# Attention steps between matmul half chunks: the two exponentials of each softmax, from neighbouring half chunks to half chunks two apart

## The chip, the cores and the metric

One Trainium2 chip, one of its cores. The metric is the device time of one execution in microseconds (us); the time before is the median of 3 runs, 785.88 us (785.31 to 786.62). A profile of one execution is there beside it.

## What is computed

For each of 8 batches and 8 heads, 32 learned queries `p` attend over 576 positions, and the 576 queries `q` then attend over the 32 packed rows. The result, 4608 tokens by 512, goes through a gated layer with a hidden width of 1536.

```python
def sm_attn(qq, kk, vv):
    s = scale * np.matmul(qq, kk.transpose(0, 1, 3, 2))
    s = s - np.max(s, axis=-1, keepdims=True)
    a = np.exp(s)
    a = a / (np.sum(a, axis=-1, keepdims=True) + 1e-09)
    return np.matmul(a, vv)
p_packed = sm_attn(p, k, v)            # first softmax: over 576 keys
out = sm_attn(q, p_packed, p_packed)   # second softmax: over 32 rows
g = x @ w_gate                         # x: out as (4608, 512)
silu = g * (1.0 / (1.0 + np.exp(-g)))
val = x @ w_val
return (silu * val @ w_out)
```

## The kernel before, in words

The attention's last product is folded into the first weights: `m_part` multiplies the packed rows (`ppts`) with the gate and value weights, and the layer's first products take the softmax weights `a2` themselves. High and low parts (`mh`/`ml`, `a2h`/`a2l`, `hh`/`hl`, `wo_h`/`wo_l`) are kept so that each product is three matmuls.

**Chunks.** The hidden width is 12 chunks (`fc`) of 128. `gv_chunk` does one chunk for half of a batch's tokens: half **A** has 256 columns, half **B** 320. This text calls the halves of chunk 9 **9A** and **9B**. In a half chunk TensorE fills two PSUM banks of the tag `gv` (the gate's, then the value's; the tag has two banks in all), ScalarE reads the first with the silu into `sg` (one buffer), VectorE multiplies the second bank by it into `hf` (in B also a 64-column rest into `t4`), ScalarE casts `hf` to `hh`, and VectorE takes the rest `hl`. The second product (`out_mm`) of a half chunk stands one chunk later. So on TensorE a half chunk is 12 matmuls into `gv` and 6 into `acc`. The first matmul of the next half chunk needs the bank which the silu reads, its seventh the bank that VectorE reads. On ScalarE the silu writes `sg` only when VectorE has read the half chunk before.

**Attention of the next batch.** While batch b is in the layer, `aux_of(b)` does the attention of batch d = b + 1, cut by `yield` into steps. A step is taken after each half's `out_mm`, so two to a chunk, in chunks 1 to 10; what is left is run off in chunk 11. In odd chunks `m_part` stands between the matmuls of half A and its `out_mm`, with two casts (`mh`) on ScalarE and two subtractions (`ml`) on VectorE.

- Step 1 and the step after: `q_scores`, the first softmax's scores in two groups. Each group has 16 small matmuls (L285; the trace shows 32), two maxima (`z`, L294) and two subtractions (`e`, L295) on VectorE, and one exponential (L298).
- Steps 4 and 5: `q_weights` sums the two groups (L308); step 5 then sends maxima and sums through DRAM (`zd`, `x`, L312 and L314, on SP's queue), and step 7 begins the join of the four parts (`y`, L319 and on).
- Steps 13 and 14: `s2_scores`, the second softmax's scores, transposed by VectorE into `s2`. From step 15 on come its two halves: maximum and subtraction (`s2_max`, L388 and L389), exponential (`s2_exp`, L393), sum and reciprocal (`s2_sums`, L400 to L402), scaling (L406), transposition and split (`s2_back`, L412 to L415).

**What sets the order.** TensorE's program is in the order of the code. On the other engines a scheduler sets it, but instructions that went through `pin` keep their order among themselves. An exponential is not issued in its step: it is put into the list `late`, and each `gv_chunk` takes one entry from the list right behind its silu:

```python
        nc.scalar.activation(sg[:, :n], pgs[0][:, :n], AF.Silu)
        if late:
            late.pop(0)()
```

Exponential and silu lie in different tables of ScalarE, so a table load (ACT_TABLE_LOAD) stands ahead of the exponential and another ahead of the next silu. Batch 0 and the attention of batch 1 run by a list written out by hand, which the change does not touch; `aux_of` serves batches 2 to 7, two softmaxes each.

Of the kernel before, what the change touches and what calls it, by code (L numbers as in the profile page):

```python
# [41 lines left out]
def tile_pack_attention_swiglu(ctx: ExitStack, tc: tile.TileContext, qT, kT, v, vq, pT, wgv, wout, out):  # L42
# [30 lines left out]
    def pin(ins):  # L73

        return tc.keep_in_program_order(ins) if steady[0] else ins

    late = []

    def ps():
        turn[0] += 1  # L80
        if wide[0] and turn[0] % 2:
            return ps_acc.tile([P, 512], F32, tag="acc", name="acc_aux")
        if wide[0]:
            return ps_gv.tile([P, 512], F32, tag="gv", name="gv_aux")
        return ps_aux.tile([P, 512], F32, tag="aux", name="aux")
# [126 lines left out]
    def s1_exp(b, par):  # L212
        t1, rs, nm = st1[b]
        nc.scalar.activation(
            t1[:, par], t1[:, par], AF.Exp, bias=nm[:, 1, par : par + 1], scale=SCALE, accum_out=rs[:, 0, par : par + 1]
        )
# [54 lines left out]
    def q_scores(b):  # L271


        k_t, p_t = kps[b]
        e = pool.tile([P, NPAR, NHP, NKQ * NP], F32, tag="s2", bufs=1, name="e1")
        z = pool.tile([P, 2, NPAR, NHP], F32, tag="z1", bufs=2, name="z1")
        sq[b] = (e, z)
        nc.gpsimd.memset(e[:, :, :, SQ:], 0.0)
        for g in range(2):
            pss = [ps(), ps()]  # L280
            for i in range(2):
                for j in range(NJ):
                    for par in range(NPAR):
                        r = slice(64 * par, 64 * par + 64)
                        nc.tensor.matmul(  # L285
                            pss[par][NP * j : NP * j + NP, i * SQ : (i + 1) * SQ],
                            p_t[r, 2 * g + i, :],
                            k_t[r, j // 2, 2 * g + i, j % 2 * SQ : j % 2 * SQ + SQ],
                            start=True, stop=True,
                        )  # L290
            hs = slice(2 * g, 2 * g + 2)
            for par in range(NPAR):
                x, m = pss[par][:, : 2 * SQ].rearrange("p (h n) -> p h n", h=2), z[:, 0, par, hs]
                pin(nc.vector.tensor_reduce(m, x, axis=AX.X, op=ALU.max))  # L294
                pin(nc.vector.tensor_tensor(  # L295
                    e[:, par, hs, :SQ], x, m.unsqueeze(2).broadcast_to([P, 2, SQ]), op=ALU.subtract
                ))
            late.append(lambda hs=hs: pin(nc.scalar.activation(e[:, :, hs, :SQ], e[:, :, hs, :SQ], AF.Exp, scale=SCALE)))  # L298
            yield

    def q_weights(b):


        e, z = sq[b]
        for g in range(2):
            yield
            hs = slice(2 * g, 2 * g + 2)
            pin(nc.vector.tensor_reduce(z[:, 1, :, hs], e[:, :, hs, :SQ], axis=AX.X, op=ALU.add))  # L308
        zv = z.rearrange("p s r h -> p s (r h)")
        x = pool.tile([P, NJ, 2, H], F32, tag="x1", bufs=1, name="x1")  # L310
        zd = dram.tile([P, 2, H], F32, tag="zd", bufs=2, name="zd")
        nc.sync.dma_start(zd, zv)  # L312
        for i in range(NJ):
            nc.sync.dma_start(x[NP * i : NP * i + NP], zd.rearrange("(j n) s h -> n j s h", j=NJ))  # L314
        for _ in range(2):
            yield
        y = pool.tile([P, 3, NJ + 1, H], F32, tag="pp", bufs=1, name="y1")
        m, t, f = y[:, 2, 0], y[:, 2, 1], y[:, 2, 2]
        pin(nc.vector.tensor_reduce(m, x[:, :, 0].rearrange("p j h -> p h j"), axis=AX.X, op=ALU.max))  # L319
        pin(nc.vector.tensor_tensor(  # L320
            y[:, 0, :NJ], x[:, :, 0], m.unsqueeze(1).broadcast_to([P, NJ, H]), op=ALU.subtract
        ))
        pin(nc.vector.tensor_tensor(y[:, 0, NJ], zv[:, 0], m, op=ALU.subtract))
        late.append(lambda: pin(nc.scalar.activation(y[:, 0], y[:, 0], AF.Exp, scale=SCALE)))
        yield
        pin(nc.vector.tensor_tensor(y[:, 1, :NJ], y[:, 0, :NJ], x[:, :, 1], op=ALU.mult))
        pin(nc.vector.tensor_reduce(t, y[:, 1, :NJ].rearrange("p j h -> p h j"), axis=AX.X, op=ALU.add))
        pin(nc.vector.tensor_scalar(f, t, 1e-9, None, op0=ALU.add))
        pin(nc.vector.reciprocal(t, f))
        pin(nc.vector.tensor_tensor(f, t, y[:, 0, NJ], op=ALU.mult))  # L330
        yield
        a1 = pool.tile([P, NPAR, NHP, NKQ, NP], F32, tag="a1", bufs=1, name="a1")
        for par in range(NPAR):
            w = e[:, par, :, :SQ]
            pin(nc.vector.tensor_tensor(
                w, w, f[:, NHP * par : NHP * par + NHP].unsqueeze(2).broadcast_to([P, NHP, SQ]), op=ALU.mult
            ))
            pin(nc.vector.transpose(
                a1[:, par].rearrange("p h k n -> p (h k n)"), e[:, par].rearrange("p h n -> p (h n)")
            ))  # L340
            yield
        sq[b] = a1
# [14 lines left out]
    def s2_tiles(b):  # L357
        st2[b] = (
            pool.tile([P, 2, NPAR, HS], F32, tag="s2", bufs=1, name="s2"),
            pool.tile([P, 3, 2 * NPAR * NBK], F32, tag="r2", bufs=1, name="r2"),  # L360
        )
# [14 lines left out]
    def s2_view(b, cs):  # L376
        s2, r2 = st2[b]
        n = NPAR * NBK
        rows = slice(cs.start * n, cs.stop * n)
        return (  # L380
            s2[:, cs].rearrange("p c r (k n) -> p (c r k) n", n=NP),
            [r2[:, i, rows] for i in range(3)],
            [P, (cs.stop - cs.start) * n, NP],
        )

    def s2_max(b, cs):
        x, (m, _, _), shape = s2_view(b, cs)
        pin(nc.vector.tensor_reduce(m, x, axis=AX.X, op=ALU.max))  # L388
        pin(nc.vector.tensor_tensor(x, x, m.unsqueeze(2).broadcast_to(shape), op=ALU.subtract))  # L389

    def s2_exp(b, cs):
        x = st2[b][0][:, cs].rearrange("p c r n -> p (c r n)")
        pin(nc.scalar.activation(x, x, AF.Exp, scale=SCALE))  # L393
# [4 lines left out]
    def s2_sums(b, cs):  # L398
        x, (m, s, r), _ = s2_view(b, cs)
        pin(nc.vector.tensor_reduce(s, x, axis=AX.X, op=ALU.add))  # L400
        pin(nc.vector.tensor_scalar(m, s, 1e-9, None, op0=ALU.add))
        pin(nc.vector.reciprocal(r, m))  # L402

    def s2_scale(b, cs):
        x, (_, _, r), shape = s2_view(b, cs)
        pin(nc.vector.tensor_tensor(x, x, r.unsqueeze(2).broadcast_to(shape), op=ALU.mult))  # L406

    def s2_back(b, c):
        s2, _ = st2[b]
        ah, al = a2[b]  # L410
        t = pool.tile([P, NPAR, HS], F32, tag="t2", bufs=1, name="t2")
        pin(nc.vector.transpose(t.rearrange("p r n -> p (r n)"), s2[:, c].rearrange("p r n -> p (r n)")))  # L412
        at = (slice(None), slice(None), slice(c * HS, (c + 1) * HS))
        nc.scalar.copy(ah[at], t)
        return lambda: pin(nc.vector.tensor_tensor(al[at], t, ah[at].bitcast(F32), op=ALU.subtract))  # L415
# [88 lines left out]
    def aux_of(b):  # L504

        d = b + 1
        if d == B:
            return
        if d < NEARLY:
            yield from s1_scores(d, False)  # L510
            for par in range(NPAR):
                late.append(lambda par=par: s1_exp(d, par))
            yield
            yield
            yield from s1_post(d)
        else:
            yield from q_scores(d)
            yield from q_weights(d)
            if d + 1 < B:
                load_k(d + 1)  # L520
            q_pack(d)
            yield
            yield
        if NEARLY <= d < B - 1:
            load_v(d + 1)
        s2_tiles(d)
        yield from s2_scores(d)
        if NEARLY <= d < B - 1:
            load_q(d + 1)
        s2_a2(d)  # L530
        order = (1, 0) if d % 2 else (0, 1)
        halves = [slice(c, c + 1) for c in order]
        for c in halves:
            s2_max(d, c)
            late.append(lambda c=c: s2_exp(d, c))
            yield
        low = lambda: None
        for c in halves:
            low()
            s2_sums(d, c)  # L540
            yield
            s2_scale(d, c)
            low = s2_back(d, c.start)
            yield
        low()

    with tc.manual_schedule(engines={mybir.EngineType.PE}):
# [308 lines left out]
```

## Time and profile before

| | |
|---|---|
| median of 3 runs | 785.88 us (785.31 to 786.62) |
| the profiled execution, its own time | 786.35 us |
| its span | 784.6 us |
| TensorE busy | 753.5 us, 96% of the span |
| VectorE busy | 453.0 us, 58% |
| ScalarE busy | 374.0 us, 48% |
| the chain that ended last | TensorE 78%, ScalarE 11%, VectorE 4% |
| granted TensorE clock, mean | 0.991 |

Rows of the timeline give the start in us, how long it took, engine, line, operation, out<-in with shapes, and the count (x2: two like instructions in a row, with the time from the first's start to the last's end); in brackets stands the idle time before and what ended it. The ends of matmuls are modelled, so distances between starts say more than their lengths. PE is TensorE, PEld its weight load, ACT ScalarE, DVE VectorE, SP the engine that issues DMAs. Batch b = 2, from which most rows are taken, starts at about 240 us.

### The profile page before, as it was taken

The page shows a single profiled execution, that of the slowest core. Times are in us where ns is not written, and L with a number is a line of the kernel's source. Part 1 is how long each engine was busy: PE and PEld are TensorE (multiplying, and loading weights), DVE is VectorE, ACT ScalarE, POOL GpSimd, SP SyncE. Part 2 cuts the span into 40 slices and gives each one's busy share as a digit, 9 for nine tenths or more (in the row PEclk, how much of TensorE's full clock was granted, in tenths as well). Part 3 has the DMA queues.
Part 4 walks back from the last instruction along what each step waited for, and adds up shares of the span by engine and source line. Part 5 has one row for each costly group of instructions (what it writes and reads, how often), then busy time and mean ns, then how long its engine had stood idle before and what let it go on. Part 6 is the DMA issues. An engine that isn't in the chain of part 4 may idle for free.

```text
span 784.6 us, 14057 instructions
## 1 busy us (share of the span) xinstructions
PE 753.5 (96%) x5750; PEld 590.1 (75%) x5750; DVE 453.0 (58%) x998; ACT 374.0 (48%) x670; POOL 2.0 (0%) x13
## 2 busy tenths in 40 slices
PE   7778999999999999999999999999999999999998
PEld 5544655678787788878777787887788787888886
DVE  5876669656575456655475545755466554753434
ACT  3656746664534536464362544555262642643331
POOL 0000000000000000000000000000000000000000
PEclk9997999999999999999999999999999999999999
DMA  9754636321111111110301202010101000010001
GB/s 351 279 215 161 209 127 251 116 64 68 61 54 27 54 69 62 54 65 3 129 1 67 68 18 111 1 55 3 69 1 55 15 3 2 1 55 1 1 1 67
DMA packets 20001, 59.08 MB, mean 75 GB/s; under 512 B 5985, under 2 KB 7009, under 8 KB 17377
## 3 DMA queue, kind: packets, MB, share of 16 engines
q1 hardware_dynamic: 19792, 58.12, 20.6%
q8 instruction: 45, 0.74, 0.4%
q14 instruction: 20, 0.16, 0.1%
q10 hardware_dynamic: 144, 0.07, 0.0%
HBM read 48.69 MB, written 9.49 MB: 74 GB/s over the span
## 4 chain that ended last, share of the span: by engine, by line
PE 78%; ACT 11%; DVE 4%; issue 2%; DVEq 0%; ACTq 0%
PE gv L469 31%; PE acc L489 25%; PE aux L180 7%; PE acc L663 5%; PE aux L489 4%; ACT L476 4%; PE gv L637 3%; PE aux L350 2%; DVE ml L422 1%; ACT sg L476 1%; ACT hh L89 1%; ACT L393 1%; ACT mh L441 1%; ACT L298 1%; PE aux L285 1%
## 5 line engine op out<-in xcount | busy, mean ns | idle before, releaser
L469 PE MATMUL gv<-a2h,ml 128*128 128x256 f32 (+1 forms) x672 | 149.6, 304 | 7.5 <-ACT sg L476 6.2
L476 ACT ACTIVATE sg<-gv 128x256 f32<-128x256 f32 (+1 forms) x168 | 68.9, 410 | 171.8 <-PE gv L469 129.6
L481 DVE TENSOR_TENSOR hf<-gv,sg 128x256 f32<-128x256 f32 x168 | 70.7, 421 | 138.5 <-PE gv L469 120.2
L469 PE MATMUL gv<-a2h,mh 128*128 128x256 f32 (+1 forms) x672 | 144.0, 296 | 0.0
L469 PE MATMUL gv<-a2l,mh 128*128 128x256 f32 (+1 forms) x672 | 143.9, 295 | 0.0
L469 PEld LDWEIGHTS gv<-a2h,ml 128*128 128x128 f32 x672 | 112.7, 188 | 32.5 <-ACT sg L476 11.4
L489 PE MATMUL acc<-wo_h,hl 128*128 128x512 f32 x336 | 136.6, 406 | 0.0
L489 PE MATMUL acc<-wo_l,hh 128*128 128x512 f32 x336 | 132.2, 393 | 0.0
L489 PE MATMUL acc<-wo_h,hh 128*128 128x512 f32 x336 | 131.6, 392 | 0.0
L89 ACT CAST hh<-hf 128x256 fp32r<-128x256 f32 x168 | 67.9, 404 | 113.4 <-DVE hf L481 113.4
L95 DVE TENSOR_TENSOR hl<-hf,hh 128x256 fp32r<-128x256 f32 x168 | 71.0, 423 | 79.0 <-ACT hh L89 78.3
L469 PEld LDWEIGHTS gv<-a2h,mh 128*128 128x128 f32 x672 | 108.4, 190 | 0.0
L469 PEld LDWEIGHTS gv<-a2l,mh 128*128 128x128 f32 x672 | 108.2, 189 | 0.0
L489 PEld LDWEIGHTS acc<-wo_h,hl 128*128 128x128 f32 x336 | 63.2, 188 | 42.5 <-issue 34.4
L489 PEld LDWEIGHTS acc<-wo_h,hh 128*128 128x128 f32 x336 | 63.1, 188 | 14.5
L422 DVE TENSOR_TENSOR ml<-aux,mh 128x512 fp32r<-128x512 f32 x92 | 59.1, 684 | 20.0 <-ACT mh L441 20.0
L489 PEld LDWEIGHTS acc<-wo_l,hh 128*128 128x128 f32 x336 | 63.3, 188 | 7.7
L180 PE MATMUL aux<-w,ppt 64*32 64x512 f32 (+1 forms) x784 | 53.3, 601 | 8.7 <-DVE w L116 8.7
L441 ACT CAST mh<-aux 128x512 fp32r<-128x512 f32 x92 | 49.2, 587 | 11.3 <-PE aux L180 8.7
L663 PE MATMUL acc<-wo_f,h 128*128 128x512 f32 x96 | 49.0, 642 | 1.7 <-DVE wo_f L116 1.7
L476 ACT ACT_TABLE_LOAD x30 | 38.5, 1283 | 10.1 <-issue 9.3
L663 PEld LDWEIGHTS acc<-wo_f,h 128*128 128x128 f32 x96 | 17.5, 198 | 22.6 <-issue 20.3
(143 smaller groups left out, 760.6 us busy)
## 6 DMA issues: line engine op xcount, KB each, us to landing
st<-in_wgv SPq DMA_DIRECT2D x12, 1024.0 KB, 4.9
k_t<-in_kT SPq DMA_DIRECT2D x16, 576.0 KB, 4.8
q_t<-in_qT SPq DMA_DIRECT2D x16, 576.0 KB, 4.9
out<-ot SPq DMA_DIRECT2D x36, 256.0 KB, 2.1
v_t<-in_vq SPq DMA_DIRECT2D x6, 1280.0 KB, 5.7
st<-in_wout SPq DMA_DIRECT2D x6, 1024.0 KB, 4.9
v_t<-in_v SPq DMA_DIRECT2D x2, 1024.0 KB, 8.4
p_t<-in_pT SPq DMA_DIRECT2D x7, 64.0 KB, 1.9
```

Of the source, the lines that this page charges most:

```text
L89: e.copy(dst, src)
L95: lo.tensor_tensor(dst_l, src, dst_h.bitcast(F32), op=ALU.subtract)
L180: nc.tensor.matmul(outs[par][32 * hp : 32 * hp + 32], lhs(r, hp), rhs(r, hp), start=True, stop=True)
L350: nc.tensor.matmul(p_p[D * par : D * par + D, NP * hp : NP * hp + NP], v_t[:, par, hp, k, :], a1[:, par, hp, k, :], start=(k == 0), stop=( ...
L422: nc.vector.tensor_tensor(*lows.pop(0), op=ALU.subtract)
L441: nc.scalar.copy(mh[at], src)
L469: nc.tensor.matmul(pg[:, :n], m_[:, g, f, s * P : (s + 1) * P], a_[:, g, off : off + n], start=(i == 0), stop=(i == 5),)
L476: nc.scalar.activation(sg[:, :n], pgs[0][:, :n], AF.Silu)
L481: nc.vector.tensor_tensor(hf, pgs[1][:, o : o + 256], sg[:, o : o + 256], op=ALU.mult)
L489: nc.tensor.matmul(acc[:, :], h_[:, c : c + P], w_[fc // 2][:, fc % 2], start=(fc == 0 and i == 0), stop=(fc == NFC - 1 and i == 2),)
L637: nc.tensor.matmul(held[i][s][:, :n], m_[:, g, f, s * P : (s + 1) * P], a_[:, g, off : off + n], start=(j == 0), stop=(j == len(todo) - 1),)
L663: nc.tensor.matmul(accs[2 * is_b + c], half(i)[:, c * P : c * P + P], wos[fc // 2][:, fc % 2], start=(fc == 0), stop=(fc == NFC - 1),)
```

## The change

In `q_scores` and `q_weights` one `yield` moves: the second group of the first softmax is now issued in step 3 and no longer in step 2 (its matmuls, maxima, subtractions and exponential), and the first sum stays in step 4. In the second softmax, step 16 now holds the sums of the first half and step 17 maximum, subtraction and exponential of the second half; before it was the other way round. Steps 15 and 18 to 21 stay. The number of steps and of instructions is the same.

```diff
@@ q_scores and q_weights
             late.append(lambda hs=hs: pin(nc.scalar.activation(e[:, :, hs, :SQ], e[:, :, hs, :SQ], AF.Exp, scale=SCALE)))
             yield
+            if g == 0:
+                yield
 
     def q_weights(b):
 
 
         e, z = sq[b]
         for g in range(2):
-            yield
+            if g:
+                yield
             hs = slice(2 * g, 2 * g + 2)
             pin(nc.vector.tensor_reduce(z[:, 1, :, hs], e[:, :, hs, :SQ], axis=AX.X, op=ALU.add))
@@ aux_of
-        for c in halves:
-            s2_max(d, c)
-            late.append(lambda c=c: s2_exp(d, c))
-            yield
-        low = lambda: None
-        for c in halves:
-            low()
-            s2_sums(d, c)
-            yield
-            s2_scale(d, c)
-            low = s2_back(d, c.start)
-            yield
+        first, second = halves
+        s2_max(d, first)
+        late.append(lambda: s2_exp(d, first))
+        yield
+        s2_sums(d, first)
+        yield
+        s2_max(d, second)
+        late.append(lambda: s2_exp(d, second))
+        yield
+        s2_scale(d, first)
+        low = s2_back(d, first.start)
+        yield
+        low()
+        s2_sums(d, second)
+        yield
+        s2_scale(d, second)
+        low = s2_back(d, second.start)
+        yield
         low()
```

Line numbers after the change are 3 higher from `s2_scores` to `aux_of` (silu L476, now L479). The instructions move as follows, at batch b = 2 (d = 3); the other batches are alike.

First, ScalarE at the second softmax, from the silu of 8B on, before:

```order
L476 ACTIVATE sg<-gv 128x320
L393 ACT_TABLE_LOAD
L393 ACTIVATE s_2829<-s_2829 128x576
L89 CAST hh<-hf 128x256
L476 ACT_TABLE_LOAD
L476 ACTIVATE sg<-gv 128x256
L393 ACT_TABLE_LOAD
L393 ACTIVATE s_2829<-s_2829 128x576
L441 CAST mh<-aux 128x512 x2
L89 CAST hh<-hf 128x256
L476 ACT_TABLE_LOAD
L476 ACTIVATE sg<-gv 128x320
```

The same place now, from the silu of 9A to that of 10B:

```order
L479 ACTIVATE sg<-gv 128x256
L89 CAST hh<-hf 128x256
L444 CAST mh<-aux 128x512 x2
L479 ACTIVATE sg<-gv 128x320
L396 ACT_TABLE_LOAD
L396 ACTIVATE s_2829<-s_2829 128x576
L89 CAST hh<-hf 128x256
L479 ACT_TABLE_LOAD
L479 ACTIVATE sg<-gv 128x256
L417 CAST a2h<-t_3029 128x2x288
L89 CAST hh<-hf 128x256
L479 ACTIVATE sg<-gv 128x320
```

The second exponential stands behind the silu of 9B and no longer behind that of 9A; the casts of 9A have no table load ahead of them. The cast `a2h` now stands ahead of the `hh` of 10A; it stood behind it. The first softmax moves in the same way: its second exponential goes from behind the silu of 2A to behind that of 2B.

Second, VectorE at the same place, from the `hl` of 8B on, before:

```order
L95 TENSOR_TENSOR hl<-hf,hh 128x256
L388 TENSOR_REDUCE r_2830<-s_2829 128x18
L389 TENSOR_TENSOR s_2829<-s_2829,r_2830 128x576
L481 TENSOR_TENSOR hf<-gv,sg 128x256
L422 TENSOR_TENSOR ml<-aux,mh 128x512 x2
L95 TENSOR_TENSOR hl<-hf,hh 128x256
L400 TENSOR_REDUCE r_2830<-s_2829 128x18
L401 TENSOR_SCALAR r_2830<-r_2830 128x18
L481 TENSOR_TENSOR hf<-gv,sg 128x256
```

and now:

```order
L95 TENSOR_TENSOR hl<-hf,hh 128x256
L403 TENSOR_REDUCE r_2830<-s_2829 128x18
L404 TENSOR_SCALAR r_2830<-r_2830 128x18
L405 RECIPROCAL r_2830<-r_2830 128x18
L484 TENSOR_TENSOR hf<-gv,sg 128x256
L95 TENSOR_TENSOR hl<-hf,hh 128x256
L391 TENSOR_REDUCE r_2830<-s_2829 128x18
L425 TENSOR_TENSOR ml<-aux,mh 128x512 x2
L392 TENSOR_TENSOR s_2829<-s_2829,r_2830 128x576
L484 TENSOR_TENSOR hf<-gv,sg 128x256
```

The subtraction for the second exponential (L389, now L392) moved behind the two `ml` of chunk 9 and ahead of the `hf` of 9B.

Third, TensorE at the first softmax. Before, the second group of scores (L285) stands between the `out_mm` that follows 1B and half 2A:

```order
L489 MATMUL acc<-wo_h,hl 128x512
L489 MATMUL acc<-wo_l,hh 128x512
L489 MATMUL acc<-wo_h,hh 128x512
L285 MATMUL aux<-k_t,p_t 32x144 x16
L469 MATMUL gv<-a2h,ml 128x256 x2
L469 MATMUL gv<-a2l,mh 128x256 x2
```

Now it stands between the `out_mm` that follows 2A and half 2B:

```order
L492 MATMUL acc<-wo_h,hl 128x512
L492 MATMUL acc<-wo_l,hh 128x512
L492 MATMUL acc<-wo_h,hh 128x512
L285 MATMUL aux<-k_t,p_t 32x144 x16
L472 MATMUL gv<-a2h,ml 128x320 x2
L472 MATMUL gv<-a2l,mh 128x320 x2
```

These 16 matmuls moved by one half chunk. Nothing else moved on TensorE, and nothing on SP's queue.

## The prediction

> **What bounds the kernel now.** I read the page first, then one stage, then the waits of TensorE.
>
> ```profile
> span 784.6 us, 14057 instructions
> PE 753.5 (96%) x5750; PEld 590.1 (75%) x5750; DVE 453.0 (58%) x998; ACT 374.0 (48%) x670; POOL 2.0 (0%) x13
> PE 78%; ACT 11%; DVE 4%; issue 2%; DVEq 0%; ACTq 0%
> 240.00:320.00 80.00, 78.87 (x665) 63.43 (x664) 45.38 (x109) 40.65 (x75) 0.20 (x1) 1.00 0.16 52
> PE gv L469 <- ACT sg L476: 6.2, 12, 1.2
> PE gv L469 <- DVE t L484: 0.7, 1, 0.7
> PE gv L637 <- DVE h L655: 0.4, 1, 0.4
> ```
>
> TensorE is busy for 96% of the span, in a stage of later batches for 78.87 of 80 us at granted clock 1.00. What it does can't get shorter by an order, so only its idle time can. The list of its waits is short: 12 times it waits for the silu (L476), 6.2 us together. Twelve is two softmaxes in each of six batches, and the timeline shows where they stand (first an undisturbed half A, then the wait at 3A, the one at 10A, and the longest one):
>
> ```profile
> 266.01 0.39 PE L489 MATMUL acc<-wo_h,hh 128*128 128x512 f32 x1
> 266.24 0.40 PE L469 MATMUL gv<-a2h,ml 128*128 128x256 f32 x2
> 267.43 0.40 PE L469 MATMUL gv<-a2h,mh 128*128 128x256 f32 x2
> 269.06 0.45 PE L469 MATMUL gv<-a2h,ml 128*128 128x320 f32 x2
> ...
> 257.98 0.39 PE L489 MATMUL acc<-wo_h,hh 128*128 128x512 f32 x1
> 258.96 0.50 PE L469 MATMUL gv<-a2h,ml 128*128 128x256 f32 x2 [0.59 <-ACT sg L476]
> 260.25 0.40 PE L469 MATMUL gv<-a2h,mh 128*128 128x256 f32 x2
> ...
> 310.31 0.40 PE L489 MATMUL acc<-wo_h,hh 128*128 128x512 f32 x1
> 311.05 0.50 PE L469 MATMUL gv<-a2h,ml 128*128 128x256 f32 x2 [0.34 <-ACT sg L476]
> 312.40 0.40 PE L469 MATMUL gv<-a2h,mh 128*128 128x256 f32 x2
> ...
> 161.17 0.39 PE L489 MATMUL acc<-wo_h,hh 128*128 128x512 f32 x1
> 162.75 0.50 PE L469 MATMUL gv<-a2h,ml 128*128 128x256 f32 x2 [1.19 <-ACT sg L476]
> 164.04 0.40 PE L469 MATMUL gv<-a2h,mh 128*128 128x256 f32 x2
> ```
>
> The idle column understates the loss, because the end of the matmul before is modelled and the first pair after a wait is slow. By starts: undisturbed, the step from the last `acc` matmul to the first `gv` is 0.23 us (266.01 to 266.24), and from there to the last pair 1.19 us. At 3A the step is 0.98 and the chunk 1.29, a loss of 0.75 + 0.10 = **0.85 us**. At 10A it is 0.74 and 1.35: 0.51 + 0.16 = **0.67 us**. In batch 1 it is 1.58 and 1.29: 1.35 + 0.10 = **1.45 us**.
>
> Why the silu is late is in ScalarE's rows at the second softmax:
>
> ```profile
> 305.60 0.38 ACT L476 ACTIVATE sg<-gv 128x256 f32<-128x256 f32 x1
> 306.00 1.28 ACT L393 ACT_TABLE_LOAD   x1
> 307.29 0.69 ACT L393 ACTIVATE s<-s 128x576 f32<-128x576 f32 x1
> 307.88 1.05 ACT L441 CAST mh<-aux 128x512 fp32r<-128x512 f32 x2
> 308.83 0.42 ACT L89 CAST hh<-hf 128x256 fp32r<-128x256 f32 x1
> 309.26 1.28 ACT L476 ACT_TABLE_LOAD   x1
> 310.56 0.44 ACT L476 ACTIVATE sg<-gv 128x320 f32<-128x320 f32 x1
> ```
>
> From the silu of 9A to that of 9B ScalarE needs 4.96 us without a gap, and the exponential before it (of 8B) had already made 9A's silu late. The silu of 9B ends at 311.00 and TensorE goes on 0.05 us later, at 311.05. Two neighbouring half chunks with an exponential ask more of ScalarE than they give it. One alone fits, as 2A shows before the change, the half chunk behind the first exponential of the first softmax:
>
> ```profile
> 252.14 0.50 PE L469 MATMUL gv<-a2h,ml 128*128 128x256 f32 x2
> 253.19 1.28 ACT L476 ACT_TABLE_LOAD   x1 [1.07 <-issue]
> 254.48 0.39 ACT L476 ACTIVATE sg<-gv 128x256 f32<-128x256 f32 x1
> 255.06 0.46 PE L469 MATMUL gv<-a2h,ml 128*128 128x320 f32 x2
> ```
>
> The load ahead of the silu starts only when the gate's bank is full (1.05 us after the chunk's start, of which 0.10 is a slow first pair), the silu ends at 254.87, and 2B starts at 255.06 without a wait. The undisturbed half A takes 269.06 - 266.24 = 2.82 us, with the slow pair 2.92, which is just 255.06. So a silu with a table load ahead of it ends some 0.95 + 1.29 + 0.39 = 2.63 us into a half A of 2.82; with the 0.05 of the handover **0.14 us are left**. That margin decides the change.
>
> **The change part by part.** It removes, adds and lengthens nothing; loads, exponentials and matmuls stay as many. What moves is checked at three places.
>
> *Second softmax (6 places).* Without the wait, 10A starts at 310.31 + 0.23 = 310.54. Up to 9A's silu (305.98) the only difference is that VectorE sums where it took a maximum. For what follows these rows give VectorE's durations, and the silu of a half B with the `hf` behind it:
>
> ```profile
> 304.61 0.75 DVE L388 TENSOR_REDUCE r<-s 128x18 f32<-128x576 f32 x1
> 305.38 0.76 DVE L389 TENSOR_TENSOR s<-s,r 128x576 f32<-128x576 f32 x1
> 308.49 1.29 DVE L422 TENSOR_TENSOR ml<-aux,mh 128x512 fp32r<-128x512 f32 x2 [2.01 <-ACT mh L441]
> 270.19 0.44 ACT L476 ACTIVATE sg<-gv 128x320 f32<-128x320 f32 x1 [1.39 <-PE gv L469]
> 271.08 0.42 DVE L481 TENSOR_TENSOR hf<-gv,sg 128x256 f32<-128x256 f32 x1 [1.40 <-PE gv L469]
> ```
>
> A half B starts 255.06 to 258.21 = 3.15 us before the next A, so 9B at 307.39, and its silu 1.13 us later (269.06 to 270.19): 308.52 to 308.96. ScalarE is free for it: behind the silu of 9A (305.98) come `hf` on VectorE (0.42) and `hh` (0.42) with some 0.05 of handover each, to 306.9, and the two `mh` in 0.95 (307.88 to 308.83), to 307.9. Then load 1.28, exponential 0.69, `hh` 0.39 less 0.10 of overlap: 311.2. The silu of 10A may load its table from 310.54 + 0.95 = 311.49 on; ScalarE is 0.25 us early. It ends at 313.16; 10B is due at 310.54 + 2.82 = 313.36. **No wait, with 0.15 left.** The exponential also needs the subtraction that now stands behind the `ml`: `hl` of 9A to 307.4, maximum to 308.1, the two `ml` from the second `mh` on to 309.3, subtraction to 310.1, ahead of the load's end (310.25) by 0.15. If it comes later, it eats first the 0.25, then the 0.15. The `hf` of 9B waits behind it until 310.1 and not 309.41 (269.06 to 271.08 is 2.02); its reader 10A needs that bank only 0.71 us after 310.54. `a2h`, now ahead of the `hh` of 10A, gets its transposition near 313.2, when the silu ends too, and the silu of 10B is not due before 314.5. So 6 x 0.67 = **4.0 us** are saved.
>
> *First softmax (6 places).* The L285 group goes to the end of 2A; TensorE pays for it there what it paid before. 2A loses a load behind it, 2B gets the exponential, and ScalarE's sequence per half chunk is that of the second softmax without the `mh` between. The load for 3A's silu then starts with 3A's own bank, and 3A has `m_part` behind it, over 1 us more before 3B. So 5 x 0.85 + 1.45 = **5.7 us** are saved. In batch 1 the two `wo_h` casts take part of this slack, by my working 0.2 is left.
>
> *What is late next.* The second sum (L308) comes behind the `ml` of chunk 3, and its DMA round trip with it:
>
> ```profile
> 166.65 0.75 DVE L308 TENSOR_REDUCE z<-e 128x4 f32<-128x576 f32 x1
> 173.34 0.21 DVE L319 TENSOR_REDUCE y<-x 128x8 f32<-128x32 f32 x1 [0.29 <-DMA x<-zd]
> 262.07 0.75 DVE L308 TENSOR_REDUCE z<-e 128x4 f32<-128x576 f32 x1
> ```
>
> In batch 1 `y` waited 0.29 us and came 5.94 us after the sum's end (167.40). In batch 2 it ended at 262.82; the `ml` ahead of it, 1.29 us, bring it to about 264.1, with TensorE 0.75 us further by then. So `y` is ready by 270.0 after the longest trip seen, and the `hf` of 4B behind it is due near 270.3 (271.08 less the gain). Cost 0; the loads of keys ahead of it on SP's queue come out later with the L285 group, by 2.8 us, and should be through by then.
>
> *The sum.* 4.0 + 5.7 = 9.7 us; the profiled execution took 786.35 us (span 784.6), so 776.6 and a span near 774.9. It stood 0.47 above the median of 785.88; as a median that is **776.2**. Bounds: by the idle column alone (6.2 us) 779.7; nothing else of TensorE's waits is touched, so not below about 775.
>
> *A rule against it.* In the trace a load starts 0.02 us after the silu (305.98, 306.00) and its exponential 1.29 us after that. The Trainium skill, in "ScalarE: Activation LUTs", section "What ACT_TABLE_LOAD costs", states 1283 ns for the load, which this trace shows to the digit, and a drain of 1380 ns with it. By that drain the silu of 10A would end at 314.5 and TensorE would wait 1.2 us there. No row here shows such a drain.
>
> **The rivals.**
>
> 1. *The margin does not hold at 10B.* The subtraction, or `hh` of 9B, is some 0.3 us later than worked out, and TensorE waits there instead. Price: 0.3 + the 0.16 of a slow restart, six times, 2.8 us: 779.0. For it: margins of 0.15 from sums of six durations. Against it: 2A above passes with no more.
> 2. *Only the first softmax gains.* The subtraction waits for both `ml` and then some, 10A's silu is as late as 9B's was: 6 x 0.67 come back, 780.2. It needs 0.9 us of lateness beyond the slack.
> 3. *Nothing gained.* A load before a lone exponential costs more than 1.28, say because what follows a silu must first drain, and the waits only move: 10A's silu 1.4 us later, 6 x (1.2 + 0.16) = 8.2 back, 784.4 to 786. Against it: the two rows at 306.00. That is where the Trainium skill's drain, named above, would lead.
> 4. *Slower.* The round trip of `x` takes VectorE's place: `y` stands ahead of the `hf` of 4B, which frees TensorE's bank for 5A. In batch 2 that bank is needed at 269.06 - 0.75 + 3.15 + 0.71 = 272.2; `y` itself, `hf`, two small ones and the rest for `t4` take some 1.2 us. So it decides from `x` landing at 271.0 on, 1 us later than the longest round trip seen. Slower by 0.2% takes (9.7 + 1.6) / 6 = 1.9 us more per batch, `x` at 272.9: near 788. Nothing in the trace shows a trip of 9 us.
>
> **How the numbers follow.** The forecast, both stalls gone: 70%, 775 to 777.5. Rival 1: 14%, rival 2: 6%, rival 3: 5%, rival 4: 3%; the rest, 2%, for a gain from waits I don't see. I give 776.2 and the range 774.5 to 780.5, which holds the forecast, rivals 1 and 2. About 0.2% (1.6 us) is what can be told from no change here. Faster by more: 0.70 + 0.14 + 0.06 + 0.02 and a little of rival 3, 0.93; the same 0.04; slower 0.03.
>
> **What would show it.** Right: the list of TensorE's waits has no L469 for the silu, the L285 group follows 2A, the load ahead of 10A's silu starts about 0.95 us after 10A and 10B follows 2.82 us after 10A. Rival 1 or 2: six waits of 10B for the silu, with the exponential starting behind its load's end. Rival 4: VectorE's L322 (L319 before) waits for `x` by more than 1 us. The forecast is wrong if starts show the twelve losses gone and the end does not move: then TensorE's order was not what set it.

## The result, and the profile after

The changed kernel takes **776.3 us** (median of 5 runs, 773.96 to 777.65), the kernel before 786.05 us (5 runs, 785.31 to 786.62). The ratio is 0.9876, with a 95% interval of 0.9856 to 0.9895: 9.75 us less. Measured once more with the experiments it was 776.98 against 785.1, ratio 0.9897 (0.9881 to 0.9912), 8.1 us less. Forecast were 776.2, and 774.5 to 780.5.

The page after, its first lines and the chain that ended last:

```profile
span 774.5 us, 14045 instructions
PE 750.5 (97%) x5750; PEld 592.1 (76%) x5750; DVE 454.8 (59%) x998; ACT 373.8 (48%) x670; POOL 2.0 (0%) x13
PE 87%; DVE 4%; ACT 2%; issue 1%; DVEq 0%; ACTq 0%
```

ScalarE's share of the chain fell from 11% to 2%, TensorE's rose from 78% to 87%; TensorE's busy time fell by 3 us, VectorE's rose by 1.8, and ScalarE's is what it was. Of the list of TensorE's waits, these are the ones in batches 1 to 7:

```profile
PE gv L472 <- DVE t L487: 0.7, 1, 0.7
PE aux L353 <- DVE a L341: 0.6, 1, 0.6
```

The row for the silu (12 times, 6.2 us) is gone. One wait of 0.65 us is new. In the list of the weight loads' waits over these batches one for the silu is left, in batch 1 ahead of 3B:

```profile
PEld gv L472 <- ACT sg L479: 0.3, 1, 0.3
```

ScalarE at the second softmax of batch 2, from the load for the second exponential on:

```profile
305.57 1.28 ACT L396 ACT_TABLE_LOAD   x1
306.86 0.69 ACT L396 ACTIVATE s<-s 128x576 f32<-128x576 f32 x1
307.45 0.39 ACT L89 CAST hh<-hf 128x256 fp32r<-128x256 f32 x1
308.07 1.28 ACT L479 ACT_TABLE_LOAD   x1 [0.23 <-issue]
309.36 0.39 ACT L479 ACTIVATE sg<-gv 128x256 f32<-128x256 f32 x1
```

and TensorE there, the last `acc` matmul and the first `gv` one of 10A and of 10B:

```profile
306.89 0.39 PE L492 MATMUL acc<-wo_h,hh 128*128 128x512 f32 x1
307.12 0.40 PE L472 MATMUL gv<-a2h,ml 128*128 128x256 f32 x2
...
309.72 0.40 PE L492 MATMUL acc<-wo_h,hh 128*128 128x512 f32 x1
309.95 0.45 PE L472 MATMUL gv<-a2h,ml 128*128 128x320 f32 x2
```

Both steps are the undisturbed 0.23 us, and 10B starts 2.83 us after 10A. ScalarE now idles for 0.23 us ahead of the load, and the silu ends at 309.75, 0.20 us before 10B. At the first softmax, the second group of scores and the step to 3B:

```profile
251.75 0.72 PE L285 MATMUL aux<-k_t,p_t 64*32 64x144 f32 x32
...
259.45 0.40 PE L492 MATMUL acc<-wo_h,hh 128*128 128x512 f32 x1
259.69 0.46 PE L472 MATMUL gv<-a2h,ml 128*128 128x320 f32 x2
```

The group takes 0.72 us as before, and the step is 0.24 us.

**Where the 10.1 us of span went.** By TensorE's starts: the first `gv` matmul of batch 1, the first scores of batches 2 and 3, and the last matmul, before

```profile
141.42 0.80 PE L469 MATMUL gv<-a2h,ml 128*128 128x256 f32 x2
246.97 1.25 PE L285 MATMUL aux<-k_t,p_t 64*32 64x144 f32 x32
334.78 1.25 PE L285 MATMUL aux<-k_t,p_t 64*32 64x144 f32 x32
780.44 0.39 PE L489 MATMUL aux<-wo_h,hh 128*128 128x512 f32 x1
```

and after:

```profile
140.21 0.80 PE L472 MATMUL gv<-a2h,ml 128*128 128x256 f32 x2
244.41 1.25 PE L285 MATMUL aux<-k_t,p_t 64*32 64x144 f32 x32
330.73 1.25 PE L285 MATMUL aux<-k_t,p_t 64*32 64x144 f32 x32
770.40 0.39 PE L492 MATMUL aux<-wo_h,hh 128*128 128x512 f32 x1
```

The profiled execution of the changed kernel came to batch 1 1.21 us earlier. Up to there the instructions of the two programs do not differ, so the change has no part in this; a second profile of the changed kernel, taken with the experiments, starts batch 1 at 141.41. Batch 1 gained 2.56 - 1.21 = 1.35 us, batch 2 1.49, and all of the rest up to the last matmul came to 10.04 - 4.05 = 5.99, four batches at 1.50. Together the changed part gained **8.83 us**.

### The profile page after: what moved, and what is told of

It is laid out like the page before. It is cut to its first block, busy times and chain, and to the rows that moved or that the text cites. A ratio compares the mean times of both kernels' runs of the same rounds, so it can differ in the third digit from the quotient of the medians.

```text
span 774.5 us, 14045 instructions
## 1 busy us (share of the span) xinstructions
PE 750.5 (97%) x5750; PEld 592.1 (76%) x5750; DVE 454.8 (59%) x998; ACT 373.8 (48%) x670; POOL 2.0 (0%) x13
## 4 chain that ended last, share of the span: by engine, by line
PE 87%; DVE 4%; ACT 2%; issue 1%; DVEq 0%; ACTq 0%
PE gv L472 35%; PE acc L492 30%; PE aux L180 8%; PE aux L492 4%; PE acc L672 4%; PE gv L646 3%; PE aux L353 2%; DVE ml L425 1%; PE aux L285 1%; ACT mh L444 1%; DVE wo_f L115 0%; DVE w L116 0%; DVE wo_f L116 0%; ACT w L112 0%; DVE h L664 0%
## 5 line engine op out<-in xcount | busy, mean ns | idle before, releaser
L479 ACT ACTIVATE sg<-gv 128x256 f32<-128x256 f32 (+1 forms) x168 | 69.1, 412 | 166.1 <-PE gv L472 131.8
L180 PE MATMUL aux<-w,ppt 64*32 64x512 f32 (+1 forms) x784 | 53.4, 602 | 7.8 <-DVE w L116 7.8
L672 PE MATMUL acc<-wo_f,h 128*128 128x512 f32 x96 | 46.8, 618 | 1.8 <-DVE wo_f L116 1.8
```

The costliest lines, as they stand in the source:

```text
L180: nc.tensor.matmul(outs[par][32 * hp : 32 * hp + 32], lhs(r, hp), rhs(r, hp), start=True, stop=True)
L672: nc.tensor.matmul(accs[2 * is_b + c], half(i)[:, c * P : c * P + P], wos[fc // 2][:, fc % 2], start=(fc == 0), stop=(fc == NFC - 1),)
```

## The experiments

Times are medians in us, ratios against the kernel before on the same chip, with 95% intervals. That kernel took 784.93 beside `e1` to `e4`, 785.1 beside `e5` to `e7`, 784.94 beside `e8`.

Since the time ahead of batch 1 varies from execution to execution (batch 1 starts between 139.83 and 142.20 us in the twelve traces), the part behind it tells the kernels apart better than the medians do. This table gives, for one trace of each, the distance from the start of batch 1's first `gv` matmul to the start of the last matmul, and the gain over the kernel before. The two kernels profiled twice repeat it to within 0.03 us.

| kernel | us | gain |
|---|---|---|
| before | 639.02 | |
| `e1` | 635.06 | 3.96 |
| `e2` | 634.05 | 4.97 |
| changed; once more | 630.19; 630.16 | 8.83; 8.86 |
| `e3` | 629.38 | 9.64 |
| `e4` | 628.97 | 10.05 |
| `e7` | 632.14 | 6.88 |
| `e5`; once more | 626.22; 626.20 | 12.80; 12.82 |
| `e6` | 630.51 | 8.51 |
| `e8` | 622.96 | 16.06 |

### One softmax at a time

The second softmax's part of the diff alone (`e1`), and the first one's alone (`e2`).

```diff
# e1: q_scores and q_weights as before; in aux_of
+        s2_sums(d, first)
+        yield
+        s2_max(d, second)
+        late.append(lambda: s2_exp(d, second))
# e2: aux_of as before; in q_scores and q_weights
             yield
+            if g == 0:
+                yield
...
-            yield
+            if g:
+                yield
```

> Only the second softmax's part of the change; the first softmax as before. Theory (two neighbouring half chunks with an exponential ask too much of ScalarE, each pair costs TensorE one wait): the six waits at 10A go, 6 x 0.67 = 4.0 us, the six at 3A stay; about 782.0 against 786.05. Rival (the gain came with the second group's score matmuls, which stand elsewhere after the change): nothing, 786. Rival (the second softmax's wait only moves from 10A to 10B when it is alone): nothing, and six waits of 0.3 us or more at 10B.

> Only the first softmax's part of the change. Theory: the six waits at 3A go, 5 x 0.85 + 1.45 = 5.7 us, less the new wait of batch 1 for the packed softmax weights (0.65 us idle in the changed kernel, some 0.75 with the restart): 4.9 to 5.7, about 780.7; the waits at 10A stay. Rival (score matmuls): all of the change's 9.75 us, 776.3.

Measured: `e1` 781.12, ratio 0.995 (0.9937 to 0.9963); `e2` 780.89, ratio 0.9945 (0.9932 to 0.9959). By the ratios that is 3.9 and 4.3 us with about 1 us of uncertainty each, 8.2 together; by starts 3.96 and 4.97, where 4.0 and 4.9 to 5.7 were expected. TensorE's waits for the silu in batches 1 to 7, of `e1`:

```profile
PE gv L469 <- ACT sg L476: 4.2, 6, 1.2
```

and of `e2`:

```profile
PE gv L472 <- ACT sg L479: 2.0, 6, 0.3
```

Each part takes away its own six waits and leaves the other six as long as they were (4.2 + 2.0 = 6.2). The new wait of 0.65 us for the packed weights (L353) stands in the list of `e2` and not in that of `e1`: it comes with the first softmax's part. The rivals fall: the score matmuls were not moved in `e1`, which gained all the same, `e2`, which moves them, did not gain all of it, and no wait appeared at 10B.

### Only the exponentials apart

Matmuls, maxima, subtractions and sums stay in their steps; an empty entry in the list puts off the second exponential.

```diff
+            if g:
+                late.append(lambda: None)
             late.append(lambda hs=hs: pin(nc.scalar.activation(e[:, :, hs, :SQ], ...
...
+            if c is halves[1]:
+                late.append(lambda: None)
             late.append(lambda c=c: s2_exp(d, c))
```

> Kernel before, but the second exponential of each softmax is taken one half chunk later by an empty entry ahead of it in the list; matmuls, maxima, subtractions and sums stay in their steps. Theory: all twelve waits go as in the changed kernel, 9 to 9.7 us, 776.3 to 777. Rival (moving the score matmuls or VectorE's work did it): little or nothing, 784 to 786.

Measured: **775.52**, ratio 0.9877 (0.9862 to 0.9891). The list of waits in batches 1 to 7 has one row left, one that the kernel before has too:

```profile
PE gv L471 <- DVE t L486: 0.7, 1, 0.7
```

So the distance between the exponentials alone brings the gain, and the new wait of batch 1 comes from the rest of the change, for it isn't here. The intervals do not tell this kernel from the changed one, but the starts do: 9.64 us against 8.83. What the change moves besides the exponentials costs it some 0.8 us.

### The pair without table loads

```diff
-            late.append(lambda hs=hs: pin(nc.scalar.activation(e[:, :, hs, :SQ], e[:, :, hs, :SQ], AF.Exp, scale=SCALE)))
+            late.append(lambda hs=hs: pin(nc.scalar.activation(e[:, :, hs, :SQ], e[:, :, hs, :SQ], AF.Abs, scale=SCALE)))
...
-        pin(nc.scalar.activation(x, x, AF.Exp, scale=SCALE))
+        pin(nc.scalar.activation(x, x, AF.Abs if steady[0] else AF.Exp, scale=SCALE))
```

The exponential of `y` is replaced in the same way. So this kernel leaves out the exponentials of batches 2 to 7.

> Kernel before with its order, but in batches 2 to 7 the exponentials are absolute values with the same shapes, which need no table load (60 loads of 1.283 us fewer; the softmax weights are then not those of the reference). Theory (what makes the pair too long is the loads): all twelve waits go without any spacing, 9.7 us or a little more because no silu waits behind a load, 775.5 to 776.5. Rival (the exponentials themselves or their place behind the silu, 0.69 us each, are enough): half of the waits or more stay, 781 or more.

Measured: 775.16, ratio 0.9874 (0.9858 to 0.9889), with the neighbouring exponentials' places left in use. The wait list has again only the row of 0.7 us, and the silu of 9B waits for TensorE, not TensorE for it:

```profile
304.83 0.44 ACT L476 ACTIVATE sg<-gv 128x320 f32<-128x320 f32 x1 [1.40 <-PE gv L469]
```

1.40 us of idle time stand where there was none. The loads made the pair too long; the two passes of 0.69 us alone fit. Spacing in `e3` gives nearly as much as doing away with the loads (9.64 and 10.05 us by starts), because it was only the pair that overran.

### How much is left at 10B

The changed kernel with the second softmax's second exponential done twice.

```diff
-        late.append(lambda: s2_exp(d, second))
+        late.append(lambda: (s2_exp(d, second), s2_exp(d, second)))
```

> Changed kernel, the second softmax's second exponential done twice (the repeat, 0.69 us, stands behind the hh of 9B; the softmax weights are then not those of the reference). It measures the margin at 10B. In the changed kernel's trace ScalarE idles 0.23 us ahead of the load for 10A's silu, and that silu ends 0.20 us before 10B starts, with 0.05 of handover: 0.38 us of slack. Theory: 0.69 - 0.38 = 0.31 us of wait and 0.16 of slow restart, six times: 2.8 us slower than the changed kernel, six waits of 10B for the silu. Rival (the slack is larger than worked out, TensorE does not go on so promptly): no wait, the same time within 0.2%.

The changed kernel beside it:

> The changed kernel unedited, beside the next ones on the same chip: ratio to the kernel before 0.9876 as measured, some 775.2 where that kernel takes 784.9.

Measured: 778.54 against 776.98, ratios 0.9915 (0.9898 to 0.9931) and 0.9897 (0.9881 to 0.9912): 1.56 us, with intervals that overlap. The trace decides. Batch 2, ScalarE and TensorE at 10A and 10B, and the wait that TensorE's weight loads show over batches 1 to 7:

```profile
308.69 0.39 ACT L89 CAST hh<-hf 128x256 fp32r<-128x256 f32 x1
308.99 0.68 ACT L396 ACTIVATE s<-s 128x576 f32<-128x576 f32 x1
309.69 1.28 ACT L479 ACT_TABLE_LOAD   x1
310.99 0.38 ACT L479 ACTIVATE sg<-gv 128x256 f32<-128x256 f32 x1
```

```profile
310.96 0.39 PE L492 MATMUL acc<-wo_h,hh 128*128 128x512 f32 x1
311.42 0.56 PE L472 MATMUL gv<-a2h,ml 128*128 128x320 f32 x2
```

```profile
PEld gv L472 <- ACT sg L479: 3.3, 7, 0.5
```

The silu ends at 311.37, and 10B starts 0.05 us later, at 311.42; its step is 0.46 us and not 0.23. So TensorE waits 0.23 us, and its first pair takes 0.10 longer (0.56 against 0.46): 0.33 us, six times 2.0 us, which is what the starts give (8.83 - 6.88 = 1.95). Six of the seven weight-load waits are these; the seventh is that of batch 1, which the changed kernel has too. Expected were 0.31 + 0.16. The slack of 0.38 us holds: the repeat begins 0.09 us before the `hh` ahead of it ends (308.69 + 0.39 = 309.08), so it adds 0.61 us and not 0.69, of which 0.61 - 0.38 = 0.23 are left as a wait. The slow restart was smaller than expected. The changed kernel stands 0.38 us of ScalarE's work from having the wait back.

### The first scores away from the other users of their banks

A wait that the list of TensorE's own waits doesn't show, since the matmul's weight load takes it; the changed kernel's row of PEld:

```profile
PEld aux L285 <- DVE ml L425: 4.6, 12, 0.4
```

These are two waits in each of six groups. The 4.6 us are not the loss, for an undisturbed group begins with 0.36 us of idle weight load as well, put down to `issue`. By starts, the first group takes 1.25 us of TensorE and the second 0.72: 0.53 us each, 3.2 us for six.

`e5` takes the first softmax's first group one half chunk later, and spaces its exponentials by an empty entry; `e6` also delays the whole second softmax.

```diff
# e5: in q_scores, to the changed kernel
+        yield
         for g in range(2):
...
+            if g:
+                late.append(lambda: None)
             late.append(lambda hs=hs: pin(nc.scalar.activation(e[:, :, hs, :SQ], ...
             yield
-            if g == 0:
-                yield
# e6: as e5, and in aux_of
+        yield
         s2_tiles(d)
         yield from s2_scores(d)
```

> Changed kernel, first softmax: the first group's scores (L285) one half chunk later, so that they no longer stand right behind the m_part whose banks they need; the second group stays in step 3, and an empty entry keeps the exponentials two half chunks apart (2A and 3A). In the changed kernel the first group takes 1.25 us on TensorE and the second 0.72. Theory: the waits of the weight load of L285 for ml go, 6 x 0.53 = 3.2 us, faster than the changed kernel by 0.3 to 0.4%. Rival (3A, with two casts and an exponential, is too much for ScalarE): new waits at 3B, up to 3 us back, no gain.

> As the one before, and the second softmax too one half chunk later (its first scores also wait for ml of the m_part ahead, 1.25 us against 0.71); its exponentials then stand in 9A and 10A, its last step is run off in chunk 11. Theory: 6.4 us over the changed kernel if no new wait comes. Rival, likelier here: at 10A the exponential, the cast a2h and the load for 10B's silu come after one another, silu of 10B about 0.2 us late and more if a2h waits for its transposition: 6 x (0.2 to 1) back, between 0.2 and 0.6% faster than the changed kernel.

Measured: `e5` **772.79**, ratio 0.9843 (0.9828 to 0.9858), 4.2 us below the changed kernel; once more 772.95, 0.9846 (0.9833 to 0.9859). Its weight loads:

```profile
PEld aux L180 <- DVE ml L426: 4.6, 12, 0.4
PEld aux L286 <- issue: 4.3, 12, 0.4
```

L286 (L285 before) no longer waits for `ml`, and the wait of batch 1 for the packed weights is gone too, so 3.2 + 0.6 of the 4.0 us that the starts give (12.80 - 8.83) are accounted for. The second softmax's L180 still has its own.

`e6` took 776.23, ratio 0.9891 (0.9872 to 0.9911): no gain over the changed kernel. TensorE's waits, and ScalarE behind the silu of 10A:

```profile
PE gv L473 <- ACT sg L480: 6.0, 6, 1.0
```

```profile
308.99 0.69 ACT L397 ACTIVATE s<-s 128x576 f32<-128x576 f32 x1
309.75 0.67 ACT L418 CAST a2h<-t 128x576 fp32r<-128x576 f32 x1
310.44 1.28 ACT L480 ACT_TABLE_LOAD   x1
311.74 0.44 ACT L480 ACTIVATE sg<-gv 128x320 f32<-128x320 f32 x1
```

This is the rival's mechanism, at a price beyond its upper end: the cast `a2h` has come between the exponential and the silu of 10B, and TensorE waits 1.0 us for that silu ahead of 11A, six times. By starts each costs 1.15 + 0.10 = 1.25 us, 7.5 us in all. The weight loads of L180 no longer wait for `ml` here, as in `e8` below, so 3.2 us were won as expected, and 12.8 + 3.2 - 7.5 = 8.5 us is the gain that the table shows. A distance of two half chunks is no help if the half chunk of the second exponential holds other work of ScalarE.

### A version that beats both

`e8` keeps the second softmax's exponentials in 8B and 9B and moves only its scores; the half whose scores come first goes first.

```diff
# to e5, in aux_of
+        yield
         s2_tiles(d)
-        yield from s2_scores(d)
+        first, second = (slice(c, c + 1) for c in range(2))
+        scores = s2_scores(d)
+        next(scores)
+        yield
+        s2_max(d, first)
+        late.append(lambda: s2_exp(d, first))
+        next(scores)
```

The `yield` ahead of it delays the step, and the two exponentials' steps follow as in the changed kernel.

> As the kernel with the first softmax's first scores later (772.8), and the second softmax's two score groups one half chunk later as well, so that the first no longer stands right behind the m_part of chunk 7; maxima, exponentials (8B and 9B), sums and all that follows stay in their steps, the half of the tokens whose scores come first is taken first. Theory: the first group's 1.25 us on TensorE become 0.72, 6 x 0.53 = 3.2 us, near 769.6, and no wait for a silu. Rival (VectorE's transpositions of the second group, now beside maximum and subtraction, hold the hf of 8B or the first exponential): part or all of it back, 771 to 773.

> The kernel with the first softmax's first scores later once more, as the measure for the one before on the same chip: ratio 0.9843 to the kernel before.

Measured: **769.08** (768.84 to 769.26), ratio **0.9797** (0.9784 to 0.9811), 3.9 us below `e5`, by starts 3.25 where 3.2 were expected. The list of TensorE's waits in batches 1 to 7 has the one row of 0.7 us, the weight loads of L180 wait for nothing but their own issue, and the first group of second scores takes 0.72 us and no longer 1.25:

```profile
PEld aux L180 <- issue: 4.4, 12, 0.4
289.73 0.72 PE L180 MATMUL aux<-q_t,ppt 64*32 64x288 f32 x16
```

## Why the prediction was right

- **What bounds it.** Twelve waits for the silu were named as the only loss that an order can change. They are gone, `e1` and `e2` take away six each, and `e3` shows that the distance of the exponentials does it.
- **The size.** Reading the loss by starts (9.7 us) and not by the idle column (6.2 us) was the step that mattered: `e3`, which moves only the exponentials, gained 9.64 us by starts, and 2.09 of them in batch 1, where 1.45 + 0.67 = 2.12 had been worked out. The changed kernel gained 8.83 by starts, and 8.1 and 9.75 in the two comparisons. From batch 2 on, a batch gained 1.49 to 1.50 us; 0.85 + 0.67 = 1.52 had been worked out.
- **What was missed.** Batch 1 of the changed kernel gained 1.35 us where 2.12 were expected. TensorE reached the packed weights (L353) earlier than VectorE had them. Before, and after:

```profile
185.50 0.83 DVE L338 STREAM_TRANSPOSE a<-e 128x640 f32<-128x640 f32 x1
186.08 2.83 PE L350 MATMUL aux<-a,v_t 128*64 128x32 f32 x80
```

```profile
183.52 0.30 PE L353 MATMUL aux<-a,v_t 128*64 128x32 f32 x2
184.47 2.52 PE L353 MATMUL aux<-a,v_t 128*64 128x32 f32 x78 [0.65 <-DVE a L341]
```

  From the start of L353 to the end of its last row it is 2.83 us before and 3.47 after, 0.64 us lost. That the wait was near could be seen before: the 80 matmuls take 2.52 in the later batches, so 2.83 already held 0.3 us of it. "Cost 0" for what is late next was wrong there by that amount. The order of VectorE shows where it fell behind. In batch 1, unlike the others, the first step of the join of `y` (L319, now L322) has gone behind the `hf` of 4B; before, and in `e3`, it stands ahead of it. Before, with `y` at 173.34, and after:

```profile
174.87 0.42 DVE L481 TENSOR_TENSOR hf<-gv,sg 128x256 f32<-128x256 f32 x1 [1.02 <-PE gv L469]
```

```profile
172.29 0.42 DVE L484 TENSOR_TENSOR hf<-gv,sg 128x256 f32<-128x256 f32 x1 [1.82 <-PE gv L472]
172.76 0.20 DVE L322 TENSOR_REDUCE y<-x 128x8 f32<-128x32 f32 x1
176.95 0.42 DVE L484 TENSOR_TENSOR hf<-gv,sg 128x256 f32<-128x256 f32 x1 [0.62 <-ACT sg L479]
```

  So the exponential of `y` and the load behind it come later on ScalarE, and the `hf` of 5A waits 0.62 us for its silu. `e2` has the same order and the same wait of L353, `e3` and `e5` have neither. No run moves `y` alone, so this cause is read from the traces and not tested. The rest of the shortfall, some 0.09 us, is a slow first pair at 3B of batch 1: its silu ends at 164.15 and 3B starts at 164.21, so the 0.2 us of slack that had been worked out there were used up.
- **Luck in the total.** The forecast of 776.2 came out within 0.1 us of the median, while the changed part gained 8.83 and not 9.7 us. In the profiled pair the 1.21 us ahead of batch 1, with which the change has nothing to do, made up for it; in the second comparison the gain was 8.1.
- **The margin at 10B.** 0.15 us of slack was worked out at the silu; the trace has 0.20 less the 0.05 of the handover, the same. The exponential did not wait for the subtraction, which ended at 306.45, 0.40 us ahead of the load's end where 0.15 had been worked out:

```profile
305.70 0.75 DVE L392 TENSOR_TENSOR s<-s,r 128x576 f32<-128x576 f32 x1
```

  Rivals 1 and 2 did not come about, and the doubled exponential shows that 0.38 us of work more would have used up the margin.
- **The load.** In `e7` the load starts 0.02 us after the exponential ends (308.99 + 0.68 to 309.69) and the silu 1.30 us after that. The drain that the Trainium skill adds to a load, in "ScalarE: Activation LUTs", section "What ACT_TABLE_LOAD costs", shows nowhere in these rows. Ahead of the lone exponential of the changed kernel the load takes no more either (305.57 to 306.86, 1.29 us), and the waits are gone; rival 3 falls with it.
- **The round trip.** `x` did come later, and VectorE waited for it by more than 1 us, which had been named as rival 4's sign, in batches 2 and 5 (1.42 and 1.52 us). In batch 2:

```profile
267.27 0.21 DVE L322 TENSOR_REDUCE y<-x 128x8 f32<-128x32 f32 x1 [1.42 <-DMA x<-zd]
267.67 0.42 DVE L484 TENSOR_TENSOR hf<-gv,sg 128x256 f32<-128x256 f32 x1 [0.19 <-PE gv L472]
```

  The wait of 1.42 us ended before the `hf` of 4B was due: `hf` still had to wait 0.19 us for TensorE. In batch 5 it starts right behind `y`, 3.14 us after the `hf` of 4A, as far behind it as in batch 2. So rival 4's place was real, and its price was nil; the sign alone did not tell it from the forecast.

## What to carry to other kernels

Where a bound engine waits for another that is half idle on average, look at what stands in two neighbouring stages of that other engine, table loads with it, and put a light stage between two heavy ones; `e6` shows that the stage must really be light. Size such a wait by the starts of the waiting engine's instructions against an undisturbed stage, not by its idle column, and look at the weight loads' waits as well: `e8` gained some 7 us more by starts (16.06 against 8.83), most of it from waits that the matmuls' own list doesn't name.

## What had not been expected of the hardware

Waits that a weight load takes may leave no idle time in the matmul's rows: for 0.33 us lost at each of six places in `e7`, and for some 0.53 us at each of twelve score groups in the changed kernel (six of L285, six of L180), TensorE's own list had no row, since the end of the matmul ahead is modelled; only PEld's list and the distances between starts show them.
